# Top-k attention into a feed-forward: the row sums of two steps share a PSUM bank, with one reciprocal and four placings every second step

## The chip, the cores and the metric

The kernel runs on one core of one Trainium2 chip. The metric is the device time of one execution in microseconds. The core has TensorE (matmuls, PE in the profile), VectorE (DVE), ScalarE (ACT), GpSimd (POOL) and SyncE (SP, which here only starts transfers). Each engine works through its own instructions in program order; they meet through semaphores. Matmuls write into PSUM, a small memory of banks that VectorE and ScalarE can read.

## The reference

Attention over 8 batches of 8 heads, 576 rows, 64 numbers a head, then a feed-forward block on the result:

```python
scores = scale * np.matmul(q, k.transpose(0, 1, 3, 2))
kth = np.partition(scores, -top_k, axis=-1)[..., -top_k:-top_k + 1]      # top_k = 32
scores = np.where(scores >= kth, scores, -1000000000.0)
attn = np.exp(scores - np.max(scores, axis=-1, keepdims=True))
attn = attn / (np.sum(attn, axis=-1, keepdims=True) + 1e-09)
x = np.matmul(attn, v)                        # heads side by side: 4608 x 512
h = np.maximum(x @ w_in, 0.0)                 # 512 -> 2048
out = h * h @ w_out                           # 2048 -> 512
```

Each row keeps its 32 largest scores, takes the softmax over them, and the row's sum divides the result. The kernel divides last: it multiplies the unnormalised weights with v and a column of ones, so that a row's sum comes out as the 65th column beside the 64 results, and then scales by the reciprocal of that column.

## The kernel before

The work is cut into 144 **steps**. A step has two halves (x = 0 and 1) of 128 rows: usually two heads of a pair with the same chunk of 128 rows. The 64 rows that are left of each head (576 is 4 x 128 + 64) go into **rest steps**, where a half holds the last 64 rows of two heads. A batch of 8 heads takes 18 steps, two of them rest steps; in most batches these are the fifth and the ninth (numbers 4 and 8 when the first is 0). Numbers of steps run through all batches, so number 4 of the second batch is step 22.

Every operation is pinned: each engine's order is the order in which the Python code calls it. The main loop runs over u, and one turn of it works on several steps at once, at different stages:

- `quads_of(u)` and `topk(u)` (lines 291, 292, 342, 346), VectorE: the 32 largest of each row of step u, by repeated search for the 8 largest and their replacement.
- `scores(u + 1)` (lines 263, 266): TensorE computes the scores of the next step into two PSUM tiles, sc_a and sc_b, and ScalarE copies both out.
- `prepare(u)` (lines 162, 199 to 209): at most of the turns, one piece of getting q, k and v of a later pair of heads ready, with copies on ScalarE.
- `invert(u - 4)` (line 436), VectorE: the reciprocals of the row sums of step u - 4, 128 x 2 numbers read from PSUM. It stands between the first and the second round of `topk(u)`.
- `place(u - 4)` (lines 452, 459), ScalarE: the results of step u - 4, scaled by the reciprocals, go from PSUM into x_tok, two copies of 128 x 64. For a rest step they are four copies of 64 x 64 into x_rem.
- `exps(u - 2)` and `turn(u - 2)` (lines 386, 395): the weights of step u - 2 on ScalarE, then their transpose by DMA.
- `pairs_of(u + 1)` on VectorE (lines 282, 283) and `copy_far(u + 1)` on ScalarE (line 298, from step 20 on): the first comparisons of the next step, and a copy of half of them for GpSimd. The next turn's line 291 reads the same PSUM tile as line 298 and comes after it.
- `dense(u, 0)` and `dense(u, 1)` (lines 533, 538, 544, 556, 561): pieces of the feed-forward block on rows whose eight heads are complete, or an idle piece (line 572) where none is ready. In the last 26 turns the first of the two takes up to two pieces.
- `products(u - 3)` (line 422), TensorE: weights times values of step u - 3 into the PSUM tile `av_ps`.

On ScalarE the order within a turn is therefore: the two copies of the scores, the preparation, the placings, the two exps, the copy of line 298, the dense pieces' copies, and the negated limits of the next turn (line 361). GpSimd works on the dropped scores (lines 307, 316, 378) and adds them by DMA (line 382).

There is one `av_ps` tile of 128 x 2 x 65 numbers, in one bank. All steps up to 141 use it in turn, so the products of step u - 3, at the end of turn u, come after the reciprocals and placings of step u - 4 in the same turn. The last two steps use another tile.

When all eight heads of a chunk are placed, `x_unit` transposes x_tok by DMA (line 496) and the block of dense pieces follows two turns later; `rem_unit` (line 502) does the same for the rests by TensorE. After the last turn come the last steps' products and placings, a matmul of one number that counts rows for which the short search was not enough (line 761), and then the dense pieces that are left.

Of the kernel before, what the change touches and what calls it, by code (L numbers as in the profile page):

```python
# [13 lines left out]
f32 = mybir.dt.float32  # L14
# [9 lines left out]
def kernel(  # L24
# [9 lines left out]
    nc = tc.nc  # L34
# [10 lines left out]
    def pin(ins):  # L45
        tc.keep_in_program_order(ins)
        return ins
# [6 lines left out]
    small = fast.enter_context(tc.tile_pool(name="small", bufs=2))  # L54
    ffp = fast.enter_context(tc.tile_pool(name="ffp", bufs=2))
    ps_sc = fast.enter_context(tc.tile_pool(name="ps_sc", bufs=1, space=PSUM))
    ps_one = fast.enter_context(tc.tile_pool(name="ps_one", bufs=1, space=PSUM))
# [26 lines left out]
            nc.gpsimd.memset(t[64 * x:64 * x + 64, 4 + x, :, 64:65], 1.0)  # L84

    flags = const.tile([128, 8 * 4 * 9, 4], f32, name="flags")
    av = ps_one.tile([128, 2, 65], f32, name="av_ps")


    pairs = [(b, pr) for b in range(B) for pr in range(H // 2)]  # L90
# [157 lines left out]
    st = {}  # L248
# [38 lines left out]
    def quads_of(u):  # L287
        d = st[u]
        cat, far, near = d["cat"], d["ps"][1][:, :, 0:QUAR], d["most"][:, 0]
        tt = nc.vector.tensor_tensor  # L290
        pin(tt(cat[:, :, 0:QUAR], far, near, op=ALU.max))  # L291
        pin(tt(cat[:, :, QUAR:HALF], far, near, op=ALU.min))  # L292
        del d["ps"]
# [30 lines left out]
    def topk(u, rounds=(0, 1, 2, 3)):  # L324
        d = st[u]
        g = u % GROUP
        if g == 0 and 0 in rounds:
            held_m["m"] = small.tile([128, GROUP, 2, 4, 8], f32, name="m", bufs=2)
        held = held_m["m"]
        m = d["m"] = [held[:, g, :, r] for r in range(4)]  # L330
        d["ends"] = held[:, g].rearrange("p x r j -> p x (r j)")[:, :, 0:32:31]
        cat = d["cat"]
        def part(r, x):
            if r == 0:
                return cat[:, x, 0:QUAR].rearrange("p (g n) -> p g n", n=18)[:, :, 0:13]
            if r == 1:
                return cat[:, x, 0:QUAR].rearrange("p (g n) -> p g n", n=6)[:, :, 1:6]
            return cat[:, x, 0:(HALF, S)[r - 2]]

        for r in rounds:  # L340
            for x in range(2):
                pin(nc.vector.max(out=m[r][:, x, :], in_=part(r, x)))  # L342
            if r == 3:
                break
            for x in range(2):
                pin(nc.vector.match_replace(out=part(r, x), in_to_replace=m[r][:, x, :], in_values=part(r, x), imm_value=NEG))  # L346
        if g == GROUP - 1 and 3 in rounds:
            f0 = 2 * (u + 1 - GROUP)
            each = held[:, :, :, :, 7].rearrange("p g x r -> p (g x) r")
            at = flags[:, f0:f0 + 2 * GROUP]  # L350
            pin(nc.gpsimd.tensor_tensor(at[:, :, 0:3], each[:, :, 3:4].broadcast_to([128, 2 * GROUP, 3]), each[:, :, 0:3], op=ALU.subtract))
            pin(nc.gpsimd.tensor_mul(at[:, :, 3], each[:, :, 3], each[:, :, 3]))
            pin(nc.gpsimd.tensor_scalar(at[:, :, 3], at[:, :, 3], scalar1=-1.0, scalar2=TINY * TINY, op0=ALU.mult, op1=ALU.add))

    def by_vector(u, x):
        return u == U - 1 or (u == U - 2 and x == 1)
# [16 lines left out]
    def drop(u, x):  # L373
        d = st[u]
        if x == 0:
            d["neg"] = negate(u, 2)
        s, byte = d["s"], gone[u % 2]
        pin(nc.gpsimd.tensor_scalar(byte[:, x, :, 1], s[:, x, :], scalar1=d["neg"][:, x, 1:2], scalar2=-HUGE, op0=ALU.add, op1=ALU.mult))  # L378
        if by_vector(u, 1) or u < EARLY:
            pin(nc.gpsimd.tensor_tensor(s[:, x, :], s[:, x, :], byte[:, x, :, :].rearrange("p n two -> p (n two)").bitcast(bf16), op=ALU.add))  # L380
        elif x == 1:
            pin(nc.gpsimd.dma_start(out=s[:, :, :].rearrange("p x n -> p (x n)"), in_=byte[:, :, :, :].rearrange("p x n two -> p (x n two)").bitcast(bf16), accum_op=ALU.add))  # L382
# [43 lines left out]

    def sums(u):
        if u < U - 2:
            return av
        if not last_two:  # L430
            last_two["ps"] = ps_sc.tile([128, 2, 512], f32, name="sc_a")
        return last_two["ps"][:, u - (U - 2), 0:130].rearrange("p (x d) -> p x d", x=2)

    def invert(u):
        r = small.tile([128, 2, 1], f32, name="rsum", bufs=4)
        pin(nc.vector.reciprocal(r[:, :, :], sums(u)[:, :, 64:65]))  # L436
        st[u]["r"] = r

    x_tok = {}
    left = {}  # L440
# [3 lines left out]
    def place(u):  # L444
        for x, (i, c, a) in enumerate(steps[u]):
            b, pr = pairs[i]
            o, r = sums(u)[:, x, :], st[u]["r"]
            if c < 4:
                if (b, c) not in x_tok:
                    x_tok[b, c] = ffp.tile([128, 512], bf16, name="x_tok", bufs=8)  # L450
                h = 2 * pr + a
                pin(nc.scalar.activation(x_tok[b, c][:, h * 64:(h + 1) * 64], o[:, 0:64], AF.Copy, scale=r[:, x, :]))
                left[b, c] = left.get((b, c), 8) - 1
                if left[b, c] == 0:
                    full.append((b, c))
            else:
                for g in range(2):
                    h, rows = 2 * pr + g, slice(64 * g, 64 * g + 64)
                    pin(nc.scalar.activation(x_rem[b % 2][rows, h * 64:(h + 1) * 64], o[rows, 0:64], AF.Copy, scale=r[rows, x, :]))
                left[b, 4] = left.get((b, 4), 4) - 1  # L460
                if left[b, 4] == 0:
                    soon_moves.append(lambda b=b: rem_unit(b))
        del st[u]
# [35 lines left out]
    def rem_unit(b):  # L499
        tp = ps_one.tile([128, KH, 128], bf16, name="gen", bufs=2)  # L500
        for kh in range(KH):
            pin(nc.tensor.transpose(tp[:, kh, :], x_rem[b % 2][:, kh * 128:(kh + 1) * 128], id_h[:, :]))
        g = b // 2

        def rest():
            for a in range(2):
                rows = slice(64 * a, 64 * a + 64)
                pin(nc.scalar.activation(xt_rem[g % 2][rows, :, (b % 2) * 64:(b % 2 + 1) * 64], tp[rows, :, 64 * a:64 * a + 64], AF.Copy))
            if b % 2:
                rem = xt_rem[g % 2]  # L510
                stores = [[(slice(64 * a, 64 * a + 64), out[(b - 1 + a) * S + 512:(b + a) * S]) for a in range(2)]]
                block(lambda kh: rem[:, kh, :], stores)
        return rest
# [128 lines left out]
    def prepare(u):  # L642
        nonlocal coming
        if not soon and coming < NP and u >= due(coming) - 4:
            assert coming < 5 or qk_left[coming - 5] == 0
            while fetches and fetches[0][0] <= coming:
                fetch(1)
            soon.extend(prep_units(coming))
            if coming + 1 < NP:
                load_pair(coming + 1)  # L650
            coming += 1
        if soon:
            soon.pop(0)()
# [16 lines left out]
    def ok(w):  # L670
        return 0 <= w < U
# [16 lines left out]
    for u in range(U):  # L688
        for x in range(2):
            if ok(u - 1) and not by_vector(u - 1, x):  # L690
                drop(u - 1, x)
        quads_of(u)
        topk(u, (0,))
        if ok(u - 4):
            invert(u - 4)
        if ok(u + 1):
            for i, c, a in steps[u + 1]:
                while coming <= i or (coming == i + 1 and soon):
                    prepare(u)
            scores(u + 1)  # L700
            both(u + 1)
        casts_next = bool(soon) and soon[0].__name__ == "values"
        for _ in range(0 if casts_next else 2 if u < 8 else 1):
            prepare(u)
        if ok(u - 4):
            place(u - 4)
        if ok(u - 2):
            exps(u - 2, 0)
            exps(u - 2, 1)
            turn(u - 2)  # L710
        fetch(10 if u < 8 else 3)
        if u >= Z:
            turn_x(u)
        topk(u, (1, 2))
        if ok(u + 1):
            pairs_of(u + 1)
            copy_far(u + 1)
            lesser(u + 1)
        topk(u, (3,))
        if casts_next:  # L720
            prepare(u)
        if by_vector(u, 1) and u < U - 1:
            early_exps(u)
        dense(u, 0)
        dense(u, 1)
        if u == U - 1:
            early_exps(u)
            exps(u - 1, 0)
        products(u - 3)
        turn_x(u)  # L730
        if w_casts and u >= 3:
            w_casts.pop(0)()
        if w_loads and u >= 1:
            w_loads.pop(0)()
# [163 lines left out]
```

## Time and profile before

| | |
|---|---|
| median of 3 runs | 940.19 us (939.16 to 942.92) |
| the profiled execution | 941.0 us, span 939.2 us |
| VectorE busy | 895.6 us, 95% of the span |
| ScalarE busy | 785.8 us, 84% |
| GpSimd busy | 776.0 us, 83% |
| TensorE busy | 685.7 us, 73% |
| mean granted TensorE clock | 0.927 |

How to read it: times are microseconds, mean durations nanoseconds. "L291" is line 291 of the kernel. A row of the timeline has start, duration, engine, line, operation, the tiles written and read, shapes, and how many instructions are merged in it; in brackets stands how long the engine was idle before it and for whom. A row of the list of waits has the waiter, whom it waited for, the total in us, how often, and the longest. A row of the table of stretches has busy us and counts of PE, PEld (weight loads), DVE, ACT and POOL, then TensorE's granted clock, the share in which the DMA engines were busy, and GB/s. A row that begins with a line and has three numbers with slashes gives the least, the median and the greatest duration in ns. The chain is the work that ended last, followed backwards; a row of it has start, length and line.

### The profile page before, as it was taken

Reading aid. Unit: us, or ns where it says so; the run is one execution under the profiler, and the core shown is the slowest. Engines: PE = TensorE matmul, PEld = TensorE weight load, DVE = VectorE, ACT = ScalarE, POOL = GpSimd, SP = SyncE. Lnnn points to the kernel's source line nnn. Section 1 sums busy time; section 2 is a strip of 40 time slices with the busy share of each in tenths; the row PEclk is TensorE's granted clock in tenths of the full one; section 3 lists DMA queues with packets and bytes.
Section 4 is the critical chain, followed back from the end, with each engine's and each line's share of the span. In section 5 each row is a group of like instructions: output and inputs, shape, how many; then the busy total and the mean of one; then the engine's idle time right before and its main releaser. Section 6 shows DMA issues by size and latency. Waiting matters only on the chain.

```text
span 939.2 us, 20939 instructions
## 1 busy us (share of the span) xinstructions
PE 685.7 (73%) x6176; PEld 434.4 (46%) x6176; DVE 895.6 (95%) x3633; ACT 785.8 (84%) x1780; POOL 776.0 (83%) x803
## 2 busy tenths in 40 slices
PE   6777676777777677776777777767777788787767
PEld 3333344444445444444454444444445455555444
DVE  6999999999999999999999999999999999999972
ACT  4677898889888988889888998888888888987884
POOL 7888889888888888888878889888898887897760
PEclk9998999899999999999989999999998998998989
DMA  5668866899998999889999999999999998886751
GB/s 140 135 156 167 176 133 131 180 196 200 200 199 182 200 205 202 188 191 194 203 189 179 191 207 200 207 184 194 189 205 193 199 211 175 167 180 135 147 115 38
DMA packets 329976, 166.29 MB, mean 177 GB/s; under 512 B 306560, under 2 KB 306560, under 8 KB 329856
## 3 DMA queue, kind: packets, MB, share of 16 engines
q1 hardware_dynamic: 311088, 92.62, 51.9%
q0 software_dynamic: 17568, 71.97, 33.8%
q8 instruction: 52, 0.85, 0.4%
q14 instruction: 68, 0.56, 0.2%
q10 hardware_dynamic: 1200, 0.30, 0.1%
HBM read 37.75 MB, written 9.44 MB: 50 GB/s over the span
## 4 chain that ended last, share of the span: by engine, by line
DVE 65%; issue 11%; ACT 9%; DMA 5%; PE 5%; POOL 2%; SPq 1%; POOLq 0%; ACTq 0%
DVE m L342 27%; DVE cat L346 17%; DVE sc_b L282 6%; DVE cat L292 5%; DVE cat L291 5%; DVE most L283 5%; DMA s<-gone_a 2%; PE sc_b L263 2%; ACT s L266 1%; ACT w_two_a L386 1%; DMA s<-gone_b 1%; PE gen L533 1%; PE dn_ps L556 1%; DVE rsum L436 1%; ACT rl L538 1%
## 5 line engine op out<-in xcount | busy, mean ns | idle before, releaser
L342 DVE MAX8 m<-cat 128x8 f32<-128x104 f32 (+3 forms) x1152 | 448.6, 433 | 0.0
L346 DVE MATCH_REPLACE8 cat<-m,cat 128x104 f32<-128x104 f32 (+2 forms) x864 | 272.1, 324 | 0.0
L307 POOL TENSOR_TENSOR cat<-s 128x576 int32<-128x576 int32 (+1 forms) x144 | 230.5, 1601 | 2.0 <-ACT s L266 2.0
L316 POOL TENSOR_TENSOR cat<-cat,most 128x576 int32<-128x576 int32 (+1 forms) x144 | 190.1, 1320 | 26.7 <-ACT most L298 14.9
L263 PE MATMUL sc_b<-qkT 64*128 64x288 f32 x512 | 109.8, 504 | 124.9 <-DVE cat L292 123.0
L533 PEld LDWEIGHTS <-w_in 128*128 128x128 bf16 x2304 | 152.4, 104 | 48.5 <-issue 27.8
L556 PE MATMUL dn_ps<-w_out,h 128*128 128x512 bf16 x576 | 165.2, 418 | 2.3 <-ACT wide L561 1.5
L533 PE MATMUL gen<-xT,w_in 128*128 128x128 bf16 x2032 | 145.3, 229 | 11.4 <-ACT xT L490 4.6
L266 ACT ACTIVATE s<-sc_b 128x576 f32<-128x576 f32 x144 | 93.3, 648 | 69.5 <-PE sc_b L263 64.4
L378 POOL TENSOR_SCALAR gone_b<-s,neg 128x576 uint8<-128x576 f32 x142 | 105.9, 746 | 30.4 <-ACT neg L361 21.1
L378 POOL TENSOR_SCALAR gone_a<-s,neg 128x576 uint8<-128x576 f32 x143 | 106.6, 746 | 28.2 <-ACT neg L361 18.6
L263 PE MATMUL sc_a<-qkT 64*128 64x288 f32 x512 | 100.6, 468 | 39.3 <-DVE most L283 28.9
L263 PEld LDWEIGHTS sc_b<-qkT 64*128 64x128 f32 x512 | 47.2, 206 | 176.2 <-issue 96.1
L266 ACT ACTIVATE s<-sc_a 128x576 f32<-128x576 f32 x144 | 91.3, 634 | 13.4 <-PE sc_a L263 12.4
L538 ACT ACTIVATE rl<-gen 128x512 f32<-128x512 f32 x143 | 85.7, 599 | 8.1 <-PE gen L533 7.2
L544 ACT ACTIVATE h<-rl 128x512 bf16<-128x512 f32 x140 | 88.2, 630 | 4.4
L422 PEld LDWEIGHTS <-wT 128*128 128x128 bf16 (+1 forms) x1600 | 59.7, 102 | 59.6 <-DMA wT<-w_two_a 24.7
L556 PEld LDWEIGHTS <-h 128*128 128x128 bf16 x576 | 54.6, 104 | 67.3 <-issue 30.7
L386 ACT ACTIVATE w_two_a<-s,neg 128x576 bf16<-128x576 f32 x96 | 69.3, 777 | 5.3 <-DMA s<-gone_a 4.3
L386 ACT ACTIVATE w_two_b<-s,neg 128x576 bf16<-128x576 f32 x95 | 68.7, 779 | 5.5 <-DMA s<-gone_b 3.9
L282 DVE TENSOR_TENSOR sc_b<-sc_a,s 128x288 f32<-128x288 f32 x144 | 66.3, 460 | 5.1 <-ACT s L266 5.0
L382 POOL DMA_DIRECT2D s<-gone_b x61 | 54.1, 888 | 20.2 <-DVE m L342 8.3
(165 smaller groups left out, 1198.4 us busy)
## 6 DMA issues: line engine op xcount, KB each, us to landing
s<-gone_a POOLq DMA_DIRECT2D x61, 576.0 KB, 4.9
s<-gone_b POOLq DMA_DIRECT2D x61, 576.0 KB, 4.7
v_raw<-in_v_dram SPq DMA_DIRECT2D x64, 128.0 KB, 3.2
out_dram<-wide SPq DMA_DIRECT2D x32, 256.0 KB, 4.2
k_raw<-in_k_dram SPq DMA_DIRECT2D x63, 128.0 KB, 3.3
q_raw<-in_q_dram SPq DMA_DIRECT2D x63, 128.0 KB, 3.2
wide<-in_moe_w_in_dram SPq DMA_DIRECT2D x8, 512.0 KB, 4.4
wide<-in_moe_w_out_dram SPq DMA_DIRECT2D x8, 512.0 KB, 4.0
```

The lines of the kernel that those rows point to most:

```text
L263: pin(nc.tensor.matmul(out=ps[j][:, x, 0:HALF], lhsT=lhsT, rhs=rhs, start=True, stop=True))
L266: pin(nc.scalar.activation(s[:, :, j * HALF:(j + 1) * HALF], ps[j][:, :, 0:HALF], AF.Copy))
L282: pin(tt(far, one[:, :, QUAR:HALF], two[:, :, QUAR:HALF], op=ALU.max))
L307: pin(tt(less, s[:, :, 0:wide].bitcast(i32), s[:, :, HALF:HALF + wide].bitcast(i32), op=ALU.add))
L316: pin(tt(less, less, d["most"][:, 0:n_h, :, :].bitcast(i32).rearrange("p h x n -> p x h n"), op=ALU.subtract))
L342: pin(nc.vector.max(out=m[r][:, x, :], in_=part(r, x)))
L346: pin(nc.vector.match_replace(out=part(r, x), in_to_replace=m[r][:, x, :], in_values=part(r, x), imm_value=NEG))
L378: pin(nc.gpsimd.tensor_scalar(byte[:, x, :, 1], s[:, x, :], scalar1=d["neg"][:, x, 1:2], scalar2=-HUGE, op0=ALU.add, op1=ALU.mult))
L386: pin(nc.scalar.activation(w_two[u % 3][:, x, 0:S], d["s"][:, x, :], AF.Exp, bias=d["neg"][:, x, 0:1]))
L533: pin(nc.tensor.matmul(out=hp[:, n * n_rows:(n + 1) * n_rows], lhsT=w_in[:, kh, (f0 + n) * 128:(f0 + n + 1) * 128], rhs=xt(kh), start=(kh ...
L538: pin(nc.scalar.activation(rl[:, :], hp, AF.Relu))
L556: pin(nc.tensor.matmul(out=op[:, :], lhsT=held["h2"][:, f, c * 128:(c + 1) * 128], rhs=w_out[:, f, :], start=(f == 0), stop=(f == NF - 1)))
```

## The change

The tile `av_ps` gets twice the size, 128 x 2 x 2 x 65 numbers, still within one bank: even steps use its first half, odd steps its second. Nothing is inverted or placed in even turns. In odd turns `invert_two(u - 5)` takes the reciprocals of both halves with one instruction of 128 x 4 numbers, and `place` is called for step u - 5 and then for u - 4. So an even step is placed one turn later than before and an odd step in the same turn as before. The last four steps (140 to 143) are inverted and placed one by one after the loop, as before.

```diff
-    av = ps_one.tile([128, 2, 65], f32, name="av_ps")
+    av = ps_one.tile([128, 2, 2, 65], f32, name="av_ps")
...
     def sums(u):
         if u < U - 2:
-            return av
+            return av[:, u % 2]
...
+    def invert_two(u):
+        r = small.tile([128, 2, 2, 1], f32, name="rsums", bufs=3)
+        pin(nc.vector.reciprocal(r[:, :, :, :], av[:, :, :, 64:65]))
+        for n in range(2):
+            st[u + n]["r"] = r[:, n]
...
-        if ok(u - 4):
-            invert(u - 4)
+        if u % 2 and ok(u - 5):
+            invert_two(u - 5)
...
-        if ok(u - 4):
+        if u % 2 and ok(u - 5):
+            place(u - 5)
             place(u - 4)
```

## The prediction

> **What bounds the kernel now.** I read the page first (busy shares and the chain that ended last), then the table of stretches, the waits, and the timeline of single steps on VectorE (DVE), ScalarE (ACT) and TensorE (PE).
>
> ```profile
> span 939.2 us, 20939 instructions
> PE 685.7 (73%) x6176; PEld 434.4 (46%) x6176; DVE 895.6 (95%) x3633; ACT 785.8 (84%) x1780; POOL 776.0 (83%) x803
> DVE 65%; issue 11%; ACT 9%; DMA 5%; PE 5%; POOL 2%; SPq 1%; POOLq 0%; ACTq 0%
> 235.00:376.00 141.00, 102.47 (x954) 65.79 (x956) 141.00 (x580) 123.32 (x285) 122.95 (x123) 0.94 0.96 198
> ```
>
> The last line is one stretch in the middle: VectorE is busy 141.00 of 141.00 us, ScalarE 123.32. VectorE sets the step there, so an instruction taken from it is worth its place in the row, as long as nothing makes it wait afterwards. What could make it wait is in the list of waits: line 291, the first comparison of a step, waits for ScalarE's copy on line 298.
>
> ```profile
> DVE cat L291 <- ACT most L298: 6.6, 7, 1.6
> DVE sc_b L282 <- ACT s L266: 5.0, 3, 3.2
> ```
>
> **Fewer reciprocals.** Before, each of 144 steps has one. After, 70 cover two steps each (0 to 139) and the last four steps keep their own: 74 in all, so 70 go. The price is not the duration but what the instruction takes of the row. The first columns are start and duration:
>
> ```profile
> 290.65 0.10 DVE L346 MATCH_VALUE_LOAD cat<-m,cat 128x8 f32 x1
> 290.72 0.27 DVE L346 MATCH_REPLACE8 cat<-m,cat 128x104 f32<-128x104 f32 x1
> 290.89 0.18 DVE L436 RECIPROCAL rsum<-av_ps 128x2 f32<-128x2 f32 x1
> 290.96 0.47 DVE L342 MAX8 m<-cat 128x8 f32<-128x120 f32 x2
> ...
> 17.39 0.44 DVE L291 TENSOR_TENSOR cat<-sc_b,most 128x288 f32<-128x288 f32 x1
> 23.79 0.44 DVE L291 TENSOR_TENSOR cat<-sc_b,most 128x288 f32<-128x288 f32 x1
> 43.04 0.45 DVE L291 TENSOR_TENSOR cat<-sc_b,most 128x288 f32<-128x288 f32 x1
> 49.50 0.45 DVE L291 TENSOR_TENSOR cat<-sc_b,most 128x288 f32<-128x288 f32 x1
> ...
> L436 DVE RECIPROCAL rsum<-av_ps x142: 147/160/195, 38.1 to 918.3; 128x2 f32<-128x2 f32 x142
> ```
>
> The reciprocal starts at 290.89 and the next instruction at 290.96: 0.07 us. The early steps say the same a second way: from 17.39 to 23.79 no reciprocal exists yet and the step takes 6.40 us; from 43.04 to 49.50 there is one and it takes 6.46. I take 0.066 x 70 = **-4.6 us**. The new reciprocal has 4 numbers a row, not 2, and the trace shows no such form. If width set the price the 70 wide ones would cost twice, and the gain would be nil; if it costs nothing, -4.6 stands. The nearest row, the load of 8 numbers at 290.65, also holds its place for 0.07 us, so I take width as free and keep 0 for the other end.
>
> [...]
>
> **Placings moved.** Even turns of the loop lose their placings (lines 452, 459), odd ones do two steps' worth. They stand on ScalarE after the copy of the scores out of sc_b (line 266) and any preparation (line 162), ahead of two exps (386) and the copy of line 298 for which VectorE waits. An even turn has that much more room, which gains nothing where VectorE was full anyway. An odd one must still reach line 298 in time. Here are an odd turn with two placings and an even one with the four half-height placings of a rest step, both with a preparation before them, each with VectorE's line 291 that follows:
>
> ```profile
> 321.62 0.65 ACT L266 ACTIVATE s<-sc_b 128x576 f32<-128x576 f32 x1
> 322.70 0.51 ACT L452 ACTIVATE x_tok<-av_ps,rsum 128x64 bf16<-128x64 f32 x2
> 323.10 1.44 ACT L386 ACTIVATE w_two_c<-s,neg 128x576 bf16<-128x576 f32 x2
> 324.47 0.41 ACT L298 ACTIVATE most<-sc_b 128x288 f32<-128x288 f32 x1
> 325.95 0.47 DVE L291 TENSOR_TENSOR cat<-sc_b,most 128x288 f32<-128x288 f32 x1
> ...
> 315.55 0.64 ACT L266 ACTIVATE s<-sc_b 128x576 f32<-128x576 f32 x1
> 316.60 1.26 ACT L459 ACTIVATE x_rem_a<-av_ps,rsum 64x64 bf16<-64x64 f32 x4
> 317.89 1.44 ACT L386 ACTIVATE w_two_b<-s,neg 128x576 bf16<-128x576 f32 x2
> 319.35 0.41 ACT L298 ACTIVATE most<-sc_b 128x288 f32<-128x288 f32 x1
> 319.85 0.47 DVE L291 TENSOR_TENSOR cat<-sc_b,most 128x288 f32<-128x288 f32 x1
> ```
>
> Two placings hold ScalarE from 322.70 to 323.10: 0.40 us. The copy ends at 324.88, 1.07 before line 291 starts. Two more placings leave 0.67: ordinary odd turns cost nothing. The rest step's turn is tight: its copy ends at 319.76, 0.09 before line 291. Rest steps are numbers 4 and 8 in nearly every batch of 18, always even, so after the change their four placings land in one odd turn together with the two of their neighbour: six. That is 0.40 on a slack of 0.09, a stall of 0.31; a turn whose forerunner placed nothing starts earlier by, as I estimate, 0.05, so I take 0.25. From turn 20 on, 12 odd turns are of this kind (27, 31, 45, 49, 63, 67, 81, 85, 99, 103, 117, 125); turn 139 gets eight placings where 138 and 139 had four each, taken as no difference.
>
> TensorE's clock makes it worse. The mean granted clock is 0.927; with a clock of one half in between, the share of time at half is (1 - 0.927) / 0.5, some 15%. A rest step's turn that met it, and below it a whole set of scores at that clock:
>
> ```profile
> core 0: 939.2 us, clock 0.927
> ...
> 179.83 1.07 PE L263 MATMUL sc_b<-qkT 64*128 64x288 f32 x4 [1.01 <-DVE cat L292]
> ...
> 181.98 0.60 ACT L162 ACTIVATE qkT<-gen 128x512 f32<-128x512 f32 x1 [0.40 <-PE gen L161]
> 182.47 1.26 ACT L459 ACTIVATE x_rem_b<-av_ps,rsum 64x64 bf16<-64x64 f32 x4
> ...
> 185.67 0.46 DVE L291 TENSOR_TENSOR cat<-sc_b,most 128x288 f32<-128x288 f32 x1 [0.61 <-ACT most L298]
> ...
> 296.43 1.33 PE L263 MATMUL sc_b<-qkT 64*128 64x288 f32 x4 [1.29 <-DVE cat L292]
> ```
>
> Four placings under a slow clock already stall VectorE 0.61; six give 1.0. At 15% that is two of the twelve: 10 x 0.25 + 2 x 1.0 = **+4.5 us**. An ordinary odd turn has 0.67 left; scores at half clock take 1.33 where the row at 294.38 (below) takes 0.76, so 0.57 more, and the wait for line 161 is 0.40: 0.57 + 0.40 - 0.67 = 0.30. Some 25 odd turns have a preparation, 15% of them is three to four: say three, **+0.9**. Gone is the stall of the even turn shown: **-0.6**.
>
> **One bank, two halves.** A product (line 422) overwrites a half whose placings must be read out. Before, each step's waits for the placings of the step ahead; after, those at the end of odd turns alone do, and the release stands on the last placing of the group, so on all six.
>
> ```profile
> 292.20 1.26 ACT L459 ACTIVATE x_rem_a<-av_ps,rsum 64x64 bf16<-64x64 f32 x4
> ...
> 293.51 0.46 PE L422 MATMUL av_ps<-vau_d,wT 128*128 128x65 bf16 x10
> ...
> 294.38 0.76 PE L263 MATMUL sc_a<-qkT 64*128 64x288 f32 x4 [0.41 <-DVE most L283]
> ```
>
> Here it does wait: placings end at 293.46, products start at 293.51, and behind them the scores are held by VectorE for 0.41. Placings that end 0.40 later just fill that gap: 0. [...]
>
> **Work that comes later.** In each batch the third chunk's x_tok, and the rests, fill up on an even step, so their transposes (line 496, on SP's queue) and rem_unit come one step later. SP passes one wT transpose and the loads of that step, all of which only wait for ScalarE; POOL's order does not change. In the last 20 turns it matters, by the order of TensorE's instructions in the two programs: the dense pieces run out one step longer, 42 idle pieces are issued in place of 40, and the row of pieces after the count matmul (line 761) grows from 11 to 14, one up and two down. That row is TensorE's alone:
>
> ```profile
> 923.85 1.05 PE gen L533 x16
> 924.90 0.86 PE dn_ps L556 x4
> 925.76 0.89 PE gen L533 x16
> ...
> 930.17 3.47 PE dn_ps L556 x16
> 933.66 0.60 ACT wide L561
> ```
>
> 0.89 + 2 x 0.86 = **+2.6 us**, with nothing beside it to hide in; if TensorE had room earlier in the tail, 0.
>
> **The sum.** -4.6 + 4.5 + 0.9 - 0.6 + 2.6 = +2.8 on the profiled execution's 941.0 us (its span and 1.8 around it): 943.8. The median of the runs, 940.19, is 0.8 below that execution, so I forecast **943.0**, +0.3%. A measurement of this kernel can tell about 0.5% from no change: 935.5 to 944.9.
>
> **Rivals.**
> - *The cover holds.* ScalarE's lead after an empty even step is larger than 0.05 and six placings fit. Speaks for it: line 291 waited for line 298 only 7 times in all; against: the start of the copy out of sc_b is set by TensorE, which waits for VectorE's line 292, and a lead of ScalarE does not move that. -4.6 - 0.6 + 2.6 gives 937.6. With the tail hidden too, 935.0: faster.
> - *A reciprocal is worth its whole 160 ns*, the median of its row: 70 x 0.160 = 11.2, that is 6.6 more, 936.4; together with the cover holding, 931.0. Against it stands the next start after 0.07. [...]
> - *Six placings always stall as in the slow-clock row* (the other side): stalls delay the exps, their transposes and the products, TensorE stands idle longer and its clock falls oftener. Twelve at 1.0 are 7.5 above my 4.5: 950.5, slower. It decides from a mean stall of 0.53 on (944.9 is 1.9 over 943.0, so 6.4 / 12).
> - *The wide reciprocal costs double*: the gain is nil, 947.6, slower.
>
> **How the numbers follow.** The forecast 0.40; the cover alone 0.10; the full duration alone 0.06; the cover with one of the two others 0.08; always stalling 0.24; double width 0.12. Faster 0.08, within 0.5% 0.56, slower 0.36. The range 936 to 948.5 takes in the double width and the milder half of the stalls, and leaves out 0.08 below and 0.12 above; the forecast's own, with stalls of 0.1 to 0.4 and the tail at 0 to 2.6, is 938.6 to 945.
>
> **What would show it.** The reciprocal's row: x70 plus four, next start still 0.07 behind it; step times of 6.10 and 6.03 by turns. Line 291's wait for line 298: above 6.6 us and more than 7 times, at odd turns of six placings; if it does not grow, my middle term is wrong. The end: 14 dense pieces behind the count matmul, and VectorE's last MAX8 no earlier by more than 2 us. A reciprocal's pitch of 0.13 would point to the width.

## The result and the profile after

| | before | after |
|---|---|---|
| median of 8 runs each, taken together | 941.15 us (938.59 to 946.38) | 946.47 us (944.34 to 950.79) |
| ratio, with 95% interval | | 1.0054 [1.0034, 1.0074] |
| the profiled execution | 941.0 us, span 939.2 | 945.6 us, span 943.7 |
| mean granted TensorE clock in it | 0.927 | 0.927 |

The changed kernel is slower by 0.54%, some 5 us. The interval leaves out "no change", but it lies across the 0.5% that I had set as the limit of what can be told. The forecast, 943.0 us, was 3.5 us too low; the range held the time. Some 1.0 of the 3.5 is the base: the forecast was built on a median before of 940.19, and the eight runs have 941.15. As a change, +2.8 was forecast and 0.54%, 5.1 us, came.

From the page of after, and from the table of the same stretch in the middle that was shown of before:

```profile
span 943.7 us, 20828 instructions
PE 686.2 (73%) x6184; PEld 435.0 (46%) x6184; DVE 893.2 (95%) x3564; ACT 785.7 (83%) x1779; POOL 776.1 (82%) x803
DVE 61%; ACT 12%; issue 10%; PE 9%; DMA 6%; POOL 1%; SPq 0%; ACTq 0%; POOLq 0%
235.00:376.00 141.00, 102.96 (x959) 65.93 (x960) 140.83 (x573) 124.18 (x286) 123.22 (x123) 0.94 0.96 198
```

VectorE still sets the step in the middle: 140.83 of 141.00 us busy, with 573 instructions in the stretch. It lost 69 instructions over the whole kernel (3633 to 3564: 70 reciprocals fewer, and one more operation of a dense piece) and 2.4 us of busy time. But the chain that ended last has moved: VectorE's share fell from 65% to 61%, ScalarE's rose from 9% to 12% and TensorE's from 5% to 9%. That tells where to look, not yet what the time came back by.

**The step.** First the row of the new line 441 in the view of one line (least, median and greatest ns), then the timeline of after (start, duration):

```profile
L441 DVE RECIPROCAL rsums<-av_ps x70: 170/198/209, 44.4 to 901.8; 128x4 f32<-128x4 f32 x70
```

```profile
191.57 0.46 DVE L291 TENSOR_TENSOR cat<-sc_b,most 128x288 f32<-128x288 f32 x1
197.61 0.45 DVE L291 TENSOR_TENSOR cat<-sc_b,most 128x288 f32<-128x288 f32 x1
203.71 0.46 DVE L291 TENSOR_TENSOR cat<-sc_b,most 128x288 f32<-128x288 f32 x1
209.73 0.47 DVE L291 TENSOR_TENSOR cat<-sc_b,most 128x288 f32<-128x288 f32 x1
216.03 0.46 DVE L291 TENSOR_TENSOR cat<-sc_b,most 128x288 f32<-128x288 f32 x1
222.07 0.44 DVE L291 TENSOR_TENSOR cat<-sc_b,most 128x288 f32<-128x288 f32 x1
...
901.83 0.19 DVE L441 RECIPROCAL rsums<-av_ps 128x4 f32<-128x4 f32 x1
901.92 0.45 DVE L342 MAX8 m<-cat 128x8 f32<-128x120 f32 x2
```

Seventy wide reciprocals; behind the last one the next instruction starts after 0.09 us, which is a little more than the 0.07 before. What counts is the turn. The turns take 6.04, 6.10, 6.02, then 6.30, then 6.04 us: an even turn without a reciprocal is some 0.07 shorter, an odd one with the wide one is as long as every turn was before, and the fourth, turn 31, is one of the twelve with six placings (four of a rest step and two of its neighbour). It is 0.20 longer than the odd turn before it.

**A turn with six placings.** ScalarE and VectorE in turn 31, and below them VectorE's same two lines in turn 33, which has no rest step:

```profile
212.58 1.26 ACT L465 ACTIVATE x_rem_b<-av_ps,rsums 64x64 bf16<-64x64 f32 x4
213.85 0.52 ACT L458 ACTIVATE x_tok<-av_ps,rsums 128x64 bf16<-128x64 f32 x2
214.26 1.44 ACT L386 ACTIVATE w_two_c<-s,neg 128x576 bf16<-128x576 f32 x2
214.49 1.44 DVE L342 MAX8 m<-cat 128x8 f32<-128x576 f32 x2
215.59 0.41 ACT L298 ACTIVATE most<-sc_b 128x288 f32<-128x288 f32 x1
...
226.84 1.42 DVE L342 MAX8 m<-cat 128x8 f32<-128x576 f32 x2
228.17 0.44 DVE L291 TENSOR_TENSOR cat<-sc_b,most 128x288 f32<-128x288 f32 x1
```

The six placings run from 212.58 to 214.26, the two exps follow, and the copy of line 298 ends at 216.00. Line 291 begins at 216.03, 0.10 after VectorE's MAX8 has ended at 215.93. In turn 33 it begins 0.09 before that end (228.17 against 228.26). So the wait that the trace books as 0.1 cost 0.2 here.

The ten turns of six placings from 27 to 103 also show what TensorE's clock does to them. Nine of them have a granted clock of 1.00 and lose 0.18 to 0.28. Turn 99 has 0.75 and takes 6.75 us, 0.65 more than 6.10. In before, turn 81, with 0.72 and two placings, takes 6.10. The two turns in the table of stretches, after first:

```profile
624.62:631.38 6.76, 5.31 (x40) 3.30 (x40) 6.22 (x27) 6.00 (x18) 4.82 (x5) 0.75 1.05 227
```

```profile
517.12:523.22 6.10, 5.15 (x40) 3.37 (x42) 6.10 (x26) 5.03 (x12) 4.94 (x5) 0.72 0.62 136
```

In e1 and e8 below, which treat these turns as after does, turn 99 loses 0.42 and 0.49 at 0.74, and the nine others 0.16 to 0.28 at 1.00.

**The waits.** Of after, and the one row of before that answers to its second:

```profile
DVE cat L291 <- ACT most L298: 6.3, 10, 1.4
PE av_ps L422 <- ACT x_tok L458: 8.9, 16, 1.3
```

```profile
PE av_ps L422 <- ACT x_tok L452: 0.8, 2, 0.5
```

Line 291's wait came 10 times, not 7, but its sum did not grow (6.6 before). The products now wait for the placings, 8.9 us in 16 times.

**The two parts of the execution.** The start of line 291 in the last step parts the loop from the end. Its rows by line, before and after, in the view of one line:

```profile
L291 DVE TENSOR_TENSOR cat<-sc_b,most x144: 426/442/479, 11.0 to 902.2; 128x288 f32<-128x288 f32 x144
```

```profile
L291 DVE TENSOR_TENSOR cat<-sc_b,most x144: 440/458/487, 10.9 to 900.3; 128x288 f32<-128x288 f32 x144
```

The loop became shorter by 1.9 us, from 902.2 to 900.3. What follows became longer, from 939.2 - 902.2 = 37.0 to 943.7 - 900.3 = 43.4 us. Here is that end, single rows of it, first in the timeline of before, then in that of after:

```profile
902.16 0.44 DVE L291 TENSOR_TENSOR cat<-sc_b,most 128x288 f32<-128x288 f32 x1
906.43 0.57 ACT L490 ACTIVATE xT<-gen 128x512 bf16<-128x512 bf16 x1
923.24 0.19 PE L761 MATMUL gen<-ones,worst 128*1 128x1 f32 x2
930.01 3.62 PE L556 MATMUL dn_ps<-w_out,h 128*128 128x512 bf16 x16
```

```profile
900.30 0.45 DVE L291 TENSOR_TENSOR cat<-sc_b,most 128x288 f32<-128x288 f32 x1
903.69 1.44 ACT L386 ACTIVATE w_two_a<-s,neg 128x576 bf16<-128x576 f32 x2 [0.71 <-DMA s<-gone_b]
905.03 0.58 ACT L544 ACTIVATE rl<-gen 128x512 f32<-128x512 f32 x1
905.64 0.63 ACT L550 ACTIVATE h<-rl 128x512 bf16<-128x512 f32 x1
906.18 0.58 ACT L567 ACTIVATE wide<-dn_ps 128x512 f32<-128x512 f32 x1
906.65 0.59 ACT L496 ACTIVATE xT<-gen 128x512 bf16<-128x512 bf16 x1
923.67 0.19 PE L768 MATMUL gen<-ones,worst 128*1 128x1 f32 x2
932.19 1.03 PE L562 MATMUL dn_ps<-w_out,h 128*128 128x512 bf16 x4
933.90 3.61 PE L562 MATMUL dn_ps<-w_out,h 128*128 128x512 bf16 x16 [0.68 <-ACT wide L567]
```

| stretch of the end, us | before | after | longer by |
|---|---|---|---|
| last line 291 to the copy of xT | 4.27 | 6.35 | 2.1 |
| copy of xT to the count matmul | 16.81 | 17.02 | 0.2 |
| count matmul to the last row of pieces | 6.77 | 10.23 | 3.5 |
| last row of pieces to the end of the span | 9.2 | 9.8 | 0.6 |

The sum is 6.4. Three things make most of it. One more up and two more downs stand behind the count matmul. The last row of downs waits 0.68 for ScalarE's copy out of dn_ps, because a down stands directly ahead of it and no up covers that copy; before, its row shows no wait. And ScalarE does three copies of dense pieces, at 905.03, 905.64 and 906.18, ahead of the copy of xT: from 905.03 to 906.65 they hold it up for 1.62 us. Before, these came earlier and the copy of xT stood directly behind the exps. The other 0.46 of the 2.1 lies ahead of the exps, which wait 0.71 for a DMA here (0.26 before).

The same two steps stand in every trace of this case. In the six kernels whose last steps are single (before, e1, e5, e6, e9, e10) the copy of xT starts some 1.35 us after the first exp, and the count matmul to the end of the last row takes 10.38. In after and in the four others that put these steps off by a turn and leave `dense` as it is (e2, e3, e4, e7) it is some 2.97 and 13.85. That is 1.6 and 3.5 us, whatever else varies.

### The profile page after: what moved, and what is told of

The parts are those of the page before. It is cut to its first block, busy times and chain, and to the rows that moved or that the text cites. A ratio compares the mean times of both kernels' runs of the same rounds, so it can differ in the third digit from the quotient of the medians.

```text
span 943.7 us, 20828 instructions
## 1 busy us (share of the span) xinstructions
PE 686.2 (73%) x6184; PEld 435.0 (46%) x6184; DVE 893.2 (95%) x3564; ACT 785.7 (83%) x1779; POOL 776.1 (82%) x803
## 4 chain that ended last, share of the span: by engine, by line
DVE 61%; ACT 12%; issue 10%; PE 9%; DMA 6%; POOL 1%; SPq 0%; ACTq 0%; POOLq 0%
DVE m L342 25%; DVE cat L346 16%; DVE sc_b L282 5%; DVE cat L291 5%; DVE cat L292 5%; DVE most L283 4%; PE sc_b L263 3%; ACT s L266 2%; DMA wT<-w_two_c 2%; PE gen L539 2%; PE dn_ps L562 2%; ACT x_tok L458 1%; DMA wT<-w_two_a 1%; ACT w_two_b L386 1%; PE sc_a L263 1%
## 5 line engine op out<-in xcount | busy, mean ns | idle before, releaser
L342 DVE MAX8 m<-cat 128x8 f32<-128x104 f32 (+3 forms) x1152 | 458.5, 450 | 0.0
L346 DVE MATCH_REPLACE8 cat<-m,cat 128x104 f32<-128x104 f32 (+2 forms) x864 | 279.3, 342 | 0.0
L562 PE MATMUL dn_ps<-w_out,h 128*128 128x512 bf16 x576 | 167.1, 420 | 4.6 <-ACT wide L567 4.6
L346 DVE MATCH_VALUE_LOAD cat<-m,cat 128x8 f32 x864 | 85.1, 98 | 0.0
L282 DVE TENSOR_TENSOR sc_b<-sc_a,s 128x288 f32<-128x288 f32 x144 | 69.0, 479 | 7.4 <-ACT s L266 7.3
L291 DVE TENSOR_TENSOR cat<-sc_b,most 128x288 f32<-128x288 f32 x144 | 66.6, 462 | 7.2 <-ACT most L298 6.3
```

What stands on the lines that cost most here:

```text
L282: pin(tt(far, one[:, :, QUAR:HALF], two[:, :, QUAR:HALF], op=ALU.max))
L562: pin(nc.tensor.matmul(out=op[:, :], lhsT=held["h2"][:, f, c * 128:(c + 1) * 128], rhs=w_out[:, f, :], start=(f == 0), stop=(f == NF - 1)))
```

## The experiments

I had two theories. **The end**: the delay by one turn costs more behind the loop than I had taken, and that is the slowdown. **The six placings**: ScalarE's lump in the turns with a rest step is the slowdown, by its stalls and by what they set off. A third question was what the wide reciprocal is worth. All kernels are versions of after; ratios are against the kernel before on the same chip. Most are made with one edit and a rule that says which pairs of steps are treated as in after:

```diff
-        if u % 2 and ok(u - 5):
+        if u % 2 and ok(u - 5) and paired(u - 5):
             invert_two(u - 5)
+        if ok(u - 4) and not paired(u - 4):
+            invert(u - 4)
...
-        if u % 2 and ok(u - 5):
+        if u % 2 and ok(u - 5) and paired(u - 5):
             place(u - 5)
+            place(u - 4)
+        if ok(u - 4) and not paired(u - 4):
             place(u - 4)
```

| kernel | what is paired | wide reciprocals | median, us | before, us | ratio, 95% |
|---|---|---|---|---|---|
| e1 | steps below 114 | 57 | 945.06 | 942.70 | 1.0015 [0.9988, 1.0041] |
| e2 | steps from 114 | 13 | 946.41 | 942.70 | 1.0045 [1.0018, 1.0071] |
| e3 | all, but two narrow reciprocals | 0 | 951.41 | 942.70 | 1.0083 [1.0054, 1.0113] |
| e4 | all without a rest step | 55 | 943.98 | 942.70 | 1.0007 [0.9984, 1.0029] |
| e5 | below 114, one step placed a turn | 57 | 940.03 | 941.92 | 0.9986 [0.9958, 1.0015] |
| e6 | below 114, without a rest step | 44 | 940.87 | 941.92 | 0.9992 [0.9969, 1.0014] |
| e7 | as e4 | 55 | 944.46 | 941.92 | 1.0018 [0.9996, 1.0041] |
| e8 | all, dense pieces taken faster at the end | 70 | 944.36 | 941.39 | 1.0028 [1.0004, 1.0051] |
| e9 | 24 to 113, without a rest step | 35 | 938.59 | 941.39 | 0.9974 [0.9950, 0.9998] |
| e10 | 24 to 113, one step placed a turn | 45 | 943.13 | 941.39 | 1.0008 [0.9983, 1.0034] |

**e1, the end as before.**

```diff
+    def paired(w):
+        return w < 114
```

> Pairs up to step 113, single steps from 114 on, so the end has 40 idle pieces and 11 pieces behind the count matmul again. Theory A (the loss is made at the end, by dense pieces that come one turn late): about 5 us below the change, that is 0 to 1.5 us below before, since at turn 118 the changed kernel's trace is 0.4 us ahead of before's. Theory B (the loss is ScalarE's six placings and their consequences in the main part, and the end only inherits it): no more than 2 us below the change.

**e2, the end alone.**

```diff
+    def paired(w):
+        return w >= 114
```

> Single steps up to 113, pairs from 114 on: only the end is changed. Theory A: 4 to 5.5 us above before (6.3 us longer from the last line 291 on, less some 1 to 1.5 us that the pairs gain on the way). Theory B: within 1.5 us of before.

The timeline of e1, then that of e2: the last line 291, the count matmul (line 775 here) and the last row of pieces.

```profile
906.96 0.43 DVE L291 TENSOR_TENSOR cat<-sc_b,most 128x288 f32<-128x288 f32 x1
928.13 0.19 PE L775 MATMUL gen<-ones,worst 128*1 128x1 f32 x2
934.89 3.62 PE L562 MATMUL dn_ps<-w_out,h 128*128 128x512 bf16 x16
```

```profile
899.70 0.44 DVE L291 TENSOR_TENSOR cat<-sc_b,most 128x288 f32<-128x288 f32 x1
921.68 0.19 PE L775 MATMUL gen<-ones,worst 128*1 128x1 f32 x2
931.92 3.61 PE L562 MATMUL dn_ps<-w_out,h 128*128 128x512 bf16 x16 [0.69 <-ACT wide L567]
```

From the count to the end of the last row it is 10.38 us in e1, as in before (923.24 to 933.63: 10.39), and 13.85 in e2, as in after (13.84). The wait of 0.69 is in e2 and not in e1. So the pairing of the last steps makes the longer end: with it alone (13 wide reciprocals, worth 0.9 us) the kernel is slower by 0.45%, 4.2 us (1.7 to 6.7 by its interval). Without it the slowdown is down to 0.15%, with no change inside the interval. The theory of the end holds. But with 57 wide reciprocals, worth 3.8 us, e1 should have stood at 0.9960, which its interval leaves out (I had expected 0 to 1.5 us below before if the end were all); something in the loop costs as much. Its own trace can't say what: its last line 291 starts at 906.96, that of after at 900.30, and 3.6 of these 6.7 us lie ahead of turn 114, up to where the two kernels do the same. Where stalls fall differed from one execution to the next (these 3.6 us, and line 282 in turn 25: 0.3 us in e9, 1.5 in e10, which do the same up to there), so the loop's length in one trace is uncertain by some us, and the causes are weighed by the runs.

**e4 and e7, rest steps apart.** The kernel was run on two chips.

```diff
+    def paired(w):
+        return not any(c == 4 for n in (w - w % 2, w - w % 2 + 1) for i, c, a in steps[n])
```

> The changed kernel, but the 15 pairs that hold a rest step are inverted and placed one by one in their own turns, so that no turn has six placings. 15 reciprocals come back (+1.0 us). If six placings cost 0.2 us a turn, as the trace of the changed kernel has it (12 turns, 2.4 us and about 1.4 us in the two worst): 1 to 2.5 us below the change. If they set off more (late transposes, a slow clock): 4 us or more below. The end keeps its 42 idle pieces.

> The version with rests apart and the changed end, once more beside the two repairs on the same chip: 3 to 5.5 us above the one with the end as before, if the end is worth that.

The timeline of e4 at turns 30 to 32, and its row of the products' wait:

```profile
203.96 0.43 DVE L291 TENSOR_TENSOR cat<-sc_b,most 128x288 f32<-128x288 f32 x1
210.06 0.43 DVE L291 TENSOR_TENSOR cat<-sc_b,most 128x288 f32<-128x288 f32 x1
216.16 0.43 DVE L291 TENSOR_TENSOR cat<-sc_b,most 128x288 f32<-128x288 f32 x1
222.19 0.43 DVE L291 TENSOR_TENSOR cat<-sc_b,most 128x288 f32<-128x288 f32 x1
```

```profile
PE av_ps L422 <- ACT x_tok L458: 2.4, 5, 1.3
```

Turns 30 and 31 take 6.10 each, 12.20 for the pair; in after they took 6.02 and 6.30, 12.32. So pairing a pair with a rest step saves 0.07 and loses 0.20. With the rest steps apart the ratio is 1.0007 and 1.0018, against 1.0054: 3.4 to 4.4 us back, each with some 3 us to either side by the intervals, for 15 reciprocals more. e4's interval lies wholly below that of after, e7's overlaps it a little. The end is still the long one in e4, so this is a second cause beside the first. How much of it is the turns themselves? In after's trace the twelve turns of six placings stand 3.8 us above 6.10 (nine of them by about 0.2 each, turns 99, 103 and 125 by 0.65, 0.28 and 1.08), in e4's 0.9, which is turn 125 alone (0.84); less the 15 x 0.067 that e4 gives up, that is 1.9. The rest, 1.5 to 2.5, I cannot place; it is no more than the two intervals allow. The products' wait fell from 8.9 to 2.4, so it comes mostly from the six placings; whether it costs time was not tried by itself.

e7 also measures the end once more, beside e6 (below) on the same chip: the two differ in the steps from 114 on alone, and e7 stands 3.6 us above e6 in the medians, 2.4 in the ratios, where I had expected 3 to 5.5, with 11 reciprocals (0.7 us) fewer to do.

**e3, two narrow reciprocals in the odd turn.**

```diff
-            invert_two(u - 5)
+            invert(u - 5)
+            invert(u - 4)
```

> The changed kernel with its placings in odd turns, but two reciprocals of 128x2 in place of one of 128x4. If a reciprocal is worth its place in VectorE's row (0.07 us), the turns become 6.03 and 6.17 and VectorE reaches its last line 291 some 4.5 us later than in the changed kernel. If the end is bound by the dense pieces (theory A), part of that is swallowed there: 2 to 4.5 us above the change. If it is worth its full 0.16 us: 11 us above. If VectorE is not what sets the turn: 0.

Its timeline:

```profile
223.06 0.44 DVE L291 TENSOR_TENSOR cat<-sc_b,most 128x288 f32<-128x288 f32 x1
229.23 0.44 DVE L291 TENSOR_TENSOR cat<-sc_b,most 128x288 f32<-128x288 f32 x1
235.26 0.44 DVE L291 TENSOR_TENSOR cat<-sc_b,most 128x288 f32<-128x288 f32 x1
241.42 0.44 DVE L291 TENSOR_TENSOR cat<-sc_b,most 128x288 f32<-128x288 f32 x1
```

The odd turns take 6.17 and 6.16, the even one 6.03. With the wide reciprocal an odd turn takes 6.10. So two narrow ones cost 0.13 and the wide one 0.07: twice the numbers cost no more place in the row. The whole gain of the change on VectorE is 70 x 0.067 = 4.7 us. The ratio rose from 1.0054 to 1.0083, 2.7 us; the intervals are too wide to tell that from 4.7.

**e6 and e9, both repairs; e9 leaves the early turns alone too.**

```diff
+    def paired(w):
+        return not any(c == 4 for n in (w - w % 2, w - w % 2 + 1) for i, c, a in steps[n]) and w < 114
```

> Both repairs: pairs without a rest step only, and only up to step 113 (44 wide reciprocals), single steps otherwise. Usual odd turns still have four placings. If the six placings and the end are all that cost: 44 x 0.067 = 2.9 us below before (1.5 to 3.5). If four placings in a turn cost too, less than the version with two in every turn gains. The version that only keeps rests apart is expected 4 us above this one, the price of the end.

```diff
+    def paired(w):
+        return 24 <= w < 114 and not any(c == 4 for n in (w - w % 2, w - w % 2 + 1) for i, c, a in steps[n])
```

> Pairs only between steps 24 and 113, none with a rest step, single steps otherwise: no six placings, the end as before, and none of the crowded early turns (7, 25) touched. 35 wide reciprocals, 35 x 0.067 = 2.3 us below before if nothing else is felt (0.5 to 3). If four placings in one turn cost as well: no gain.

In the view of line 441 of e9:

```profile
L441 DVE RECIPROCAL rsums<-av_ps x35: 159/169/179, 200.6 to 725.5; 128x4 f32<-128x4 f32 x35
```

e9 is 2.8 us faster than before in the medians; 35 x 0.067 gives 2.3. It is the only kernel of the series whose interval lies below 1, and just so (0.9998); as the best of ten it may owe part of that to chance. e6, which pairs nine more, came out at 0.9992 with 1 inside, some 0.8 us by the ratio where I had expected 1.5 to 3.5. Why e6 is no better than e9 is not settled: in the timelines line 282 stalls in turn 25 by 1.6 us in e6 and by 0.3 in e9, but by 1.5 in e10 (below), which does the same as e9 up to there. The intervals of e6 and e9 overlap over most of their width.

**e8, the end worked off faster.** In the last three turns the first call of `dense` may take three pieces.

```diff
-        N = 2 if (u >= U - 26 and x == 0) or len(ups) + len(downs) > 24 else 1
+        N = 3 if U - 3 <= u < U and x == 0 else 2 if (u >= U - 26 and x == 0) or len(ups) + len(downs) > 24 else 1
```

> The changed kernel, with up to three dense pieces in place of two in the first half of the last three turns: four pieces are drawn ahead of the count matmul, 10 stand behind it (14 in the change, 11 before). If the late pieces are what the end costs: the stretch from the count matmul to the last matmul falls from 13.85 to some 9.5 us, and the time by 2 to 4 us against the change. If ScalarE cannot take the copies of the drawn pieces earlier: the stretch ahead of the count matmul grows by as much, and the time is as with the change.

Its timeline:

```profile
923.62 0.19 PE L768 MATMUL gen<-ones,worst 128*1 128x1 f32 x2
932.39 3.61 PE L562 MATMUL dn_ps<-w_out,h 128*128 128x512 bf16 x16 [0.69 <-ACT wide L567]
```

From the count to the end of the last row it is 12.38 us instead of 13.84. I had expected 9.5: eleven pieces stand behind the count, not ten, and the first three of them met a granted clock of 0.61 (923.6 to 928.0). The ratio fell to 1.0028, by 2.5 us, but with overlapping intervals. So the pieces behind the count are part of the longer end; that they can be had back in time without undoing the pairing is likely and not shown. The wait of 0.69 stays.

**e5 and e10, one step placed in each turn.** If the lump of placings is the trouble, spreading it should help: the pair is inverted together, but its odd step is placed one turn later. e5 pairs the steps below 114, e10 those from 24 to 113.

```diff
-        if u % 2 and ok(u - 5):
+        if ok(u - 5) and paired(u - 5):
             place(u - 5)
+        if ok(u - 4) and not paired(u - 4):
             place(u - 4)
```

> Pairs up to step 113 and single steps from 114 on, as in the first experiment, with the same 57 wide reciprocals; but each turn places one step: the even step of a pair in the odd turn of its reciprocal, the odd step in the turn after. So ScalarE has two placings in every turn (four for a rest step) and never six, and the end has 40 idle pieces. If the odd turns' lump on ScalarE is what took the gain of the main part: 57 x 0.067 = 3.8 us below before, say 2 to 4.5. If the lump is innocent and the main part's stalls come by chance: like the first experiment, 0 to 3 us above before.

> Pairs between steps 24 and 113, rests among them, but one step placed in each turn; single steps otherwise. 45 wide reciprocals, 3.0 us below before (1 to 4) if a later placing of the odd steps costs nothing.

e5 gave 0.9986, e10 1.0008, both with 1 inside their intervals. Neither reached what I expected: the 3.8 us of e5 lie just inside its interval, the 3.0 of e10 outside. e5's profiled execution took 946.77 us, far above its median, so I read nothing from its trace. So placing each odd step a turn later has not been shown to help, and in e10 something gives the gain back; what, stays open.

## Why the prediction was right or wrong, step by step

| term, us | forecast | measured | from |
|---|---|---|---|
| 70 reciprocals | -4.6 | -4.7 | turns of 6.03 and 6.10; e3 |
| six placings, 12 turns | +4.5 | +3.8 above 6.10, +2.9 against e4, +1.5 against before | starts of line 291 |
| other stalls of the loop | +0.9 - 0.6 | +1.4 | starts of line 291 |
| the loop in all | +0.2 | -1.9 | last line 291 |
| the end | +2.6 | +6.4 | rows of the end |
| in all | +2.8 | +4.5 in the traces | spans |

The middle rows are worked out from the 143 distances between starts of line 291: what each is above the undisturbed turn (6.40 in turns 0 to 3, 6.46 to turn 18, 6.10 from turn 19 on, less 0.067 where a reciprocal is gone). Before, these stalls sum to 12.3 us, after to 15.2.

- *The reciprocals*: right, price and width both. The rival of the full 160 ns and that of the double width fell with e3 and the turns.
- *The placings*: the mechanism was right, at the turns named: ScalarE's copy of line 298 ends last, and an undisturbed turn of six loses 0.2, where I took 0.25. The slow clock makes it worse, as I had it, but by less on the whole: turn 99 lost 0.42 to 0.65 in after, e1 and e8, and two such turns of e3 1.1 and 0.4 above its 6.17 (turns 27 and 103, at 0.77 and 0.74), where I had 1.0. In after only one of the ten turns up to 103 met it. Turn 125 is a case of its own. Before, it stalled by 2.3 us without the change, so against before the twelve turns cost only 1.5. The six kernels whose steps from 114 on are single all have 2.15 to 2.71 above 6.10 there, the six others 0.84 to 1.26, e4 and e7 without six placings among them: the change takes something away there that I had not seen, and why is open. Against e4 the twelve turns cost 2.9, so the term was sized too high. My test, that line 291's wait for line 298 must grow above 6.6 us, was badly set: the sum stayed because stalls of before went (turns 26, 74 and 75 among them) as new ones came, and because a wait of 0.1 in that list cost 0.2, as in turn 31. "The cover holds" is refuted by e4; "always stalling" at 1.0 a turn too, with 3.8 / 12 = 0.3. That the clock falls after stretches in which TensorE is idle more the traces do show: up to 936 us the granted clock falls 33 times in before, and TensorE was busy 37% of the 2 us ahead of a fall, 70% on average of all 2-us stretches at 1.00 (38% and 71% in after). But it did not fall oftener: 32 times in after.
- *Ordinary odd turns and stalls that go*: other turns in all got 1.4 longer, where I had +0.3 net. Which of them stall changed from one execution to the next (turn 25 of e9 and e10, above), so I claim no more than the size. For the loop as a whole the runs are the better measure: e1, which has the end of before, stands at 1.0015, some 1.4 us [-1.1, +3.9], and the forecast's +0.2 lies within that. That it came so near is partly luck: the placings were taken too high and the other stalls too low.
- *One bank, two halves*: the "0" for the products failed as a statement on the wait (8.9 us in 16 times). No run shows that it costs time.
- *The end*: this is the step that failed, "0.89 + 2 x 0.86 = +2.6 us, with nothing beside it to hide in". The three pieces were right (14 behind the count). What I left out: the last block's downs wait 0.68 for a copy that before had time; 0.6 more follow the last matmuls; and ahead of the count the same delay puts three dense copies in ScalarE's last turn in front of the copy of xT, on which TensorE waits. I had followed TensorE's order of instructions in the last turns, but not ScalarE's. e2 carries it: the end alone costs 4.2 us. The 0.6 behind the last matmuls I can't explain.

So the forecast was low because the end was sized at about half: e2's 4.2 us and the 0.9 that its 13 reciprocals save make 5.1, where I had 2.6. That is 2.5 us, as much as the 2.3 by which the change was missed (5.1 against 2.8); the other 1.0 of the 3.5 is the median before. All this is within what the runs can tell, some 2 to 3 us. e4 and e7 put the placings, with all they set off, at 3.4 to 4.4 us net, and at 4.4 to 5.4 with the 1.0 for 15 reciprocals put back: near the 4.5 of the forecast, and more than the 2.9 that the turns themselves show in one trace.

## What to carry to other kernels

An instruction taken from the engine that sets the step is worth what the turn gets shorter by (here 0.067 us, not the 160 ns of its row), and two of them merged cost one place here (odd turns of 6.10 us against 6.17 with two); but the work that hangs on it becomes a lump on another engine, so pair only where that engine's slack takes the lump, and leave single what is already tight. Work that is put off by one turn was paid here where a backlog is worked off alone: follow every engine's order in the last turns, not the one engine that ends last. Here the two versions that keep both rules came out at 0.9974 (e9) and 0.9992 (e6), a gain that is barely shown, and the change as made loses 0.54%.

## What the runs showed of the hardware

- A short wait cost VectorE more than its idle time in after. Undisturbed (turn 33), line 291 starts 0.09 us before the MAX8 ahead of it has ended; when it waits (turn 31), it starts 0.10 after that end, and the turn is 0.20 longer than turn 29, the odd turn before it.
- A reciprocal of 128x4 numbers from PSUM has a median of 198 ns in after and 169 in e9, against 160 for 128x2 before, and takes the same place, 0.067 us a turn (odd turns 6.10, even ones 6.03).
- Taken by half microseconds up to 936 us, the granted clock of before is 1.00 in 1568, 0.50 in 239 and between in the 65 others. At a granted clock of 0.72 a turn of before (81) takes the same 6.10 us as others; with six placings, turn 99 of after takes 6.75 at 0.75, where the nine other such turns up to 103, at 1.00, take 6.28 to 6.38.
- The same kernel's time went with the granted clock: e5's executions go from 936.49 us at a mean clock of 0.936 to 949.19 at 0.913, and its four longest are the four with the lowest clocks (0.913 to 0.923). In the nine other versions the two go together less strictly (a correlation of -0.36 to -0.70, against -0.91 in e5). With a change worth 2 to 5 us, six to twelve executions a kernel gave intervals of about 0.25% to either side, and no finer question was settled here.
